# The first biases of a selective-attention kernel: two copies instead of one, a subtraction on GpSimd, and the first scores issued earlier

## The chip, the cores and the metric

The kernel runs on one core of one Trainium2 chip. The metric is the device time of one execution in microseconds (us). The core's engines are TensorE (PE in the profile; PEld is its weight load), VectorE (DVE), ScalarE (ACT), GpSimd (POOL) and SyncE (SP, which only issues DMAs here). Each works through its own instructions in program order, and they wait for each other by semaphores.

## What is computed

Two blocks follow each other. The first is causal attention with a learned decay: per batch and head the positive part of `s` is summed up along the sequence, and the difference of two sums is a bias on the score.

```python
B, H, S, D = 8, 8, 576, 64
scores = q @ k.transpose(0, 1, 3, 2) / np.sqrt(D)
cum = np.cumsum(np.maximum(s, 0.0), axis=-1)
bias = -(cum[:, :, :, None] - cum[:, :, None, :])
scores = np.where(causal, -1e9, scores + np.minimum(bias, 0.0))
attn = softmax(scores)
attn_out = attn @ v
```

The second block is a mixture of eight experts (512 to 1024 to 512, relu) on the 4608 tokens that the first yields; a gate decides per token whether it keeps the expert of the token before it.

## The kernel before

**Stages.** `attention` goes over 32 pairs of heads (8 batches with 4 pairs each), then `experts` goes over units of sorted tokens. The change lies in what `attention` does ahead of the loop and in the first turn of the loop.

**The bias.** Inside the softmax the part of the bias that depends on the query alone cancels, so the kernel adds only a term per key: `cum[key]` less the sum at a fixed middle column. There are two groups of queries (`GROUPS`: columns 0 to 320 and 320 to 576), each with a middle column of its own (`MIDS`), so that the exponents stay small. Lines 289 to 312 make all these terms once for all 64 heads: VectorE takes the positive part of `s` (L289), sums it up (L291), and subtracts the middle column for each group (`rel`, L299: 384 columns for the first group, 576 for the second). PE turns `rel` into columns of 128 keys (L302: three turnings for the first group, four for the second), and two small products (L307) put the last 64 keys, the tail, beside them. All of it goes into one PSUM tile `bps` (480 columns). One copy on VectorE (L310) brings it to `bias` in SBUF, and a memset (L312) masks half a block. ACT's exponentials (L339, L357) take columns of `bias` as their per-partition bias.

**PSUM.** The pool `ps_s` has three buffers of two banks (tag "s"). `bps` takes the first, and the scores of the units take them in turn. A buffer is taken again when what reads it is done.

**A pair.** `scores(n, u)` writes k q for one of three units (`UNITS`; each has 512 columns for each of two heads, L330). `weights` lets ACT take the exponentials of one piece of a unit into the SBUF tile `sc` (L339), and lets GpSimd zero what the causal mask hides (L345). `tail_scores` and `tail` (L351, L357) do the same for the last 64 keys; `seen_tail` (L361) masks them on VectorE. `gate_parts` (L370) and `beside_v` (L375, L376) put the gate's logits beside v. `rows` (L408 to L413) multiplies the weights of the pair before by v, and divides by the sum.

**Order.** The program's order is that of the Python code, written out by hand. Ahead of the loop it is: load pairs 0 to 2 (`load`, L255, issued on SP's queue, pair 0's k on ACT's), `spin(18)`, the bias, `tail_scores(0)`. `spin(n)` multiplies the identity by itself n times (L286) into a bank that nobody reads; each is two matmul records in the profile. In turn n of the loop: load pair n + 3, then for each unit its scores and its weights, then `rows(n - 1)` (in the first turn `spin(8)`), `tail_scores(n + 1)`, `gate_parts(n)`, `beside_v(n)`.

Of the kernel before, what the change touches and what calls it, by code (L numbers as in the profile page):

```python
# [10 lines left out]
F32 = mybir.dt.float32  # L11
I32 = mybir.dt.int32
Act = mybir.ActivationFunctionType
Alu = mybir.AluOpType
# [4 lines left out]
P = 128  # L19
B, H, S, DH = 8, 8, 576, 64  # L20
# [4 lines left out]
NPAIR = B * HP  # L25
NF = S // P
TS = NF * P
TL = S - TS
# [19 lines left out]
MASKED = -1e9  # L48
SUM_MIN, SUM_MAX = 1e-20, 1e20
GROUPS = ((0, 5 * TL), (5 * TL, S))  # L50
MIDS = (5 * TL // 2, 7 * TL)


UNITS = (
    ((0, 0, 0, 5 * TL), (3, 1, 3 * P, S)),
    ((0, 1, 5 * TL, S), (1, 1, 5 * TL, S)),
    ((2, 0, 2 * P, 5 * TL), (2, 1, 5 * TL, S), (1, 0, P, 5 * TL)),
)
# [9 lines left out]
def kernel(  # L68
# [33 lines left out]
    with ExitStack() as main:  # L102
# [51 lines left out]
        last = sort.group((6, 7), xs)  # L154

        attention(tc, q, kz, vz, vx, s, w_gate, w_local, ident, lg, recs, const, new_x, plan)
        tables = sort.tables()
        check = in_range(main.enter_context(tc.tile_pool(name="g_sb", bufs=1)), nc, recs, sort.total, sort.ones, out_of)
# [51 lines left out]
def attention(ctx, tc, q, kz, vz, vx, s, w_gate, w_local, ident, lg, recs, keep, new_x, plan):  # L210
# [14 lines left out]
    nc = tc.nc  # L225
    mm, tr = nc.tensor.matmul, nc.tensor.transpose
    scale = 1.0 / math.sqrt(DH)
    BH = B * H

    def pool(name, bufs, **kw):  # L230
        return ctx.enter_context(tc.tile_pool(name=name, bufs=bufs, **kw))
# [3 lines left out]
    once = pool("once", 1)  # L235
    ps_s = pool("ps_s", 3, space=PSUM)
# [3 lines left out]
    banks = [ps_o.tile([P, 512], F32, name=f"o{g}", tag=f"o{g}") for g in range(2)]  # L240
    COLUMNS = ((0, 3), (3, NB))
    TAIL = 2 * VW
# [3 lines left out]
    ins, raw, scs, xs = {}, {}, {}, {}  # L246

    def load(n, other=nc.sync):
        if n >= NPAIR:
            return  # L250
        b, hp = divmod(n, HP)
        ins[n] = [p_in.tile([P, S], F32, name="q"), *(p_in.tile([P, TS + 2 * TL], F32, name=x) for x in ("k", "vt")),
                  p_vx.tile([P, NB, VW], F32, name="v")]
        for t, x, eng in zip(ins[n], (q[b][:, hp], kz[n], vz[n], vx[n]), (nc.sync, other, nc.sync, nc.sync)):
            eng.dma_start(t, x)  # L255

    tmp = ctx.enter_context(ExitStack())
    t_in = tmp.enter_context(tc.tile_pool(name="t_in", bufs=1))
    s_sb = t_in.tile([BH, S], F32, name="s_sb")
# [3 lines left out]
    ones = t_in.tile([BH, S], F32, name="ones")  # L263
# [8 lines left out]
    for h in range(2):  # L272
        d = slice(h * DH, h * DH + DH)
# [5 lines left out]
    for h in range(2):  # L279
        d = slice(h * DH, h * DH + DH)  # L280
# [3 lines left out]
    def spin(n):  # L284
        for i in range(n):
            mm(banks[1][:, :P], lhsT=ident, rhs=ident, start=True, stop=True)  # L286

    spin(18)
    nc.vector.tensor_scalar_max(s_sb, s_sb, 0.0)  # L289
    cum = t_in.tile([BH, S], F32, name="cum")  # L290
    nc.vector.tensor_tensor_scan(cum, ones, s_sb, 0.0, op0=Alu.mult, op1=Alu.add)  # L291


    bps = ps_s.tile([P, 2, 512], F32, name="bps", tag="s")[:, 0]
    bias_of, at = {}, 0
    for g, (q0, q1) in enumerate(GROUPS):
        n = -(-q1 // P) * P if g == 0 else S
        rel = t_in.tile([BH, n], F32, name=f"rel{g}")
        nc.vector.tensor_scalar(rel, cum[:, :n], cum[:, MIDS[g] : MIDS[g] + 1], None, Alu.subtract)  # L299
        for c, a in enumerate(range(0, TS, P)):  # L300
            if a + P <= n:
                tr(bps[:, at : at + BH], rel[:, a : a + P], ident[:BH, :BH])  # L302
                bias_of[c, g] = at
                at += BH
    tail_bias = at
    for h in range(2):
        mm(bps[h * TL : h * TL + TL, at : at + NPAIR], lhsT=rel[:, TS:], rhs=ident[:BH, h:BH:2], start=True, stop=True)  # L307
    at += NPAIR
    bias = once.tile([P, at], F32, name="bias")
    nc.vector.tensor_copy(bias, bps[:, :at])  # L310
    at = bias_of[2, 0]
    nc.vector.memset(bias[TL:, at : at + BH], MASKED)  # L312
    tmp.close()
    p_sc = pool("p_sc", 2, reuse_waits="tile")

    def scores(n, u):

        qb, kb = ins[n][:2]
        ps = raw[u] = ps_s.tile([P, 2, 512], F32, name="ps", tag="s")
        scs[n, u] = p_sc.tile([P, 2, sum(z - a for _, _, a, z in UNITS[u])], F32, name=f"sc{u}")  # L320
        runs = []
        for c, g, a, z in UNITS[u]:
            if runs and runs[-1][0] == c and runs[-1][2] == a:
                runs[-1][2] = z
            else:
                runs.append([c, a, z, PIECE[c, g][1]])
        for c, a, z, at in runs:
            for h in range(2):
                d = slice(DH * h, DH * h + DH)
                mm(ps[:, h, at : at + z - a], lhsT=kb[d, c * P : c * P + P], rhs=qb[d, a:z],  # L330
                   start=True, stop=True)

    def weights(n, *pieces):

        for c, g in pieces:
            u, at, a, z = PIECE[c, g]
            for h in range(2):
                i = bias_of[c, g] + 2 * n + h
                nc.scalar.activation(scs[n, u][:, h, at : at + z - a], raw[u][:, h, at : at + z - a], Act.Exp,  # L339
                                     bias=bias[:, i : i + 1], scale=scale)  # L340
            if min(c * P + P, S) <= z and (c, g) in PIECE:
                at += c * P - a
                if at >= 0:
                    x = scs[n, u][:, :, at : at + P]
                    nc.gpsimd.affine_select(out=x, in_=x, compare_op=Alu.is_ge, fill=0.0, base=0,  # L345
                                            pattern=[[0, 2], [1, P]], channel_multiplier=-1)

    def tail_scores(n):
        for h in range(2):
            d = slice(DH * h, DH * h + DH)  # L350
            mm(banks[1][d, TAIL : TAIL + TL], lhsT=ins[n][1][:, TS:][:, d], rhs=ins[n][0][:, TS:], start=True, stop=True)  # L351

    def tail(n):

        sc = scs[n, "tail"] = p_sc.tile([P, TL], F32, name="tail")
        i = tail_bias + n
        nc.scalar.activation(sc, banks[1][:, TAIL : TAIL + TL], Act.Exp, bias=bias[:, i : i + 1], scale=scale)  # L357

    def seen_tail(n):
        x = scs[n, "tail"]  # L360
        nc.vector.scalar_tensor_tensor(x, x, 3e38, seen, Alu.min, Alu.mult)  # L361
# [3 lines left out]
    def gate_parts(n):  # L365

        m = P // 2
        for c in range(NB):
            for j in range(0, P, m):
                mm(gates[j : j + m, c], lhsT=ins[n][2][:, c * P + j : c * P + j + m], rhs=wz[:, n % HP],  # L370
                   start=True, stop=True)

    def beside_v(n):
        v = ins[n][3]
        nc.vector.tensor_copy(v[:, :, 1 : E + 2], gates[:, :, 0])  # L375
        nc.vector.tensor_copy(v[:, :, VW - E - 2 : VW - 1], gates[:, :, 1])  # L376
# [38 lines left out]
    def logits(b):  # L415
        x = xs.pop((b, "x"))
        for t0, t1, m in ((1, NB, P), (0, 1, TL)):
            part = x[:m, t0:t1, :XI].rearrange("p t (a w) -> p t a w", w=2 * HW)
            pair = keep.tile([P, NF, HP, E + 1], F32, name="pair")[:m, : t1 - t0]
            nc.vector.tensor_tensor(pair, part[:, :, :, : E + 1], part[:, :, :, 2 * HW - E - 1 :], op=Alu.add)  # L420
            nc.vector.tensor_reduce(lg[:m, b * NB + t0 : b * NB + t1, :], pair.rearrange("p t a e -> p t e a"),
                                    axis=AX, op=Alu.add)

    def bank(n):
        t = ps_s.tile([P, 2, 512], F32, name="bank", tag="s")
        return [t[:, i] for i in range(n)]

    tail_scores(0)
    for n in range(NPAIR + 1):
        load(n + 3)  # L430
        if n < NPAIR:
            for u, pieces in enumerate((((0, 0), (3, 1)), ((0, 1), (1, 1)), ((2, 0), (2, 1), (1, 0)))):
                scores(n, u)
                for piece in pieces:
                    weights(n, piece)
                    if piece == (0, 0):
                        tail(n)
                for f in plan.pop((n, 3 + u), ()):
                    f(bank)
            seen_tail(n)  # L440
        for f in plan.pop((n, 0), ()):
            f(bank)
        if n:
            rows(n - 1, 1)
            rows(n - 1, 0)
        else:
            spin(8)

        if n + 1 < NPAIR:
            tail_scores(n + 1)  # L450
        if n < NPAIR:
            gate_parts(n)
            beside_v(n)
        if n and n % HP == 0:
            logits(n // HP - 1)
        for half in (1, 2):
            for f in plan.pop((n, half), ()):
                f(bank)
# [899 lines left out]
```

## Time and profile before

| | us |
|---|---|
| median of 5 executions | 803.54 |
| lowest and highest of them | 801.27 and 804.6 |
| the profiled execution | 804.4 |
| its span, first to last instruction | 802.7 |
| PE busy | 784.6 |
| DVE busy | 338.7 |
| ACT busy | 237.0 |
| POOL busy | 175.1 |

How to read the lines: a group of instructions has its line in the source, its engine and operation, the tiles that it writes and reads (out<-in), shapes, count, busy time, the mean of one in ns, and the idle time of its engine just before, with what ended that. A timeline row has its start, its length, the same names, and in brackets the idle time before it. The chain of waits is the work that ended last, followed back from the end: each piece is what released the next one, or what stood before it on its engine. "issue" is time in which the profile shows nothing that was waited for.

### The profile page before, as it was taken

To read this page: it belongs to the slowest core of one execution; us is meant where nothing else is said; L and a number is where in the kernel's file an instruction comes from. 1 tells how busy PE (TensorE), PEld (TensorE's weight loads), DVE (VectorE), ACT (ScalarE), POOL (GpSimd) and SP (SyncE) were. 2 spreads that over 40 slices of the span, in tenths; PEclk is the share of its full clock that TensorE was granted. 3 is DMA by queue.
4 is the path that set the end of the run, shared out by engine and by line. 5 is a ranking of instruction groups with operands and counts; after the bars stand their busy time and mean duration, and the time that the engine had idled before them with its cause. 6 is when DMAs were issued, how large, how long until landed. Compare 5 with 4: busy or idle time off the path is not lost.

```text
span 802.7 us, 18230 instructions
## 1 busy us (share of the span) xinstructions
PE 784.6 (98%) x7078; PEld 562.5 (70%) x7078; DVE 338.7 (42%) x1228; ACT 237.0 (30%) x611; POOL 175.1 (22%) x329
## 2 busy tenths in 40 slices
PE   9999999999999989999999999999999999999996
PEld 8989888888788854863677537774477745676762
DVE  2233443444447658424372253622545225436000
ACT  5767766756654201111111111111111111111110
POOL 3423345454443141101110012101111011011001
PEclk9999999999999999999999999999999999999998
DMA  9486679887483389957999369993699946994001
GB/s 310 167 275 192 194 225 318 286 263 234 152 276 140 127 271 410 395 192 249 341 376 403 135 236 339 391 405 111 239 359 394 361 136 242 365 411 189 22 14 43
DMA packets 64146, 204.47 MB, mean 255 GB/s; under 512 B 8270, under 2 KB 8302, under 8 KB 64049
## 3 DMA queue, kind: packets, MB, share of 16 engines
q1 hardware_dynamic: 55008, 172.41, 60.6%
q0 software_dynamic: 8896, 30.47, 10.0%
q8 instruction: 58, 0.95, 0.5%
q10 hardware_dynamic: 144, 0.33, 0.2%
q14 instruction: 40, 0.32, 0.1%
HBM read 179.93 MB, written 23.76 MB: 254 GB/s over the span
## 4 chain that ended last, share of the span: by engine, by line
issue 57%; PE 29%; POOL 4%; DVE 4%; DMA 2%; POOLq 1%; another core or an unknown queue 1%; SPq 1%; ACT 0%; DVEq 0%
PE o L408 12%; PE ps L330 10%; POOL out_dram L1249 2%; PE o L370 2%; POOL xg L1184 2%; PE hp L1231 2%; DVE xT L1088 1%; DMA xg<-x_rows 1%; POOLq L1159 1%; SPq L808 1%; PE o L351 1%; DMA s_sb<-in_s_dram 1%; PE bank L947 1%; DVE x L413 0%
## 5 line engine op out<-in xcount | busy, mean ns | idle before, releaser
L1088 DVE STREAM_TRANSPOSE xT<-xg 32x128 f32<-32x128 f32 x576 | 174.2, 302 | 173.7 <-PE hp L1231 97.2
L1244 PE MATMUL yp<-w,hT 128*128 128x512 f32 (+1 forms) x528 | 218.0, 596 | 0.0
L1231 PE MATMUL hp<-xT,w 128*128 128x256 f32 (+1 forms) x1088 | 192.5, 337 | 3.3 <-issue 2.9
L1231 PEld LDWEIGHTS hp<-xT,w 128*128 128x128 f32 x1088 | 172.1, 191 | 27.5 <-issue 11.2
L339 ACT ACTIVATE sc<-ps,bias 128x256 f32<-128x256 f32 (+3 forms) x448 | 156.5, 482 | 62.7 <-PE ps L330 60.7
L1244 PEld LDWEIGHTS yp<-w,hT 128*128 128x128 f32 (+1 forms) x528 | 90.7, 181 | 115.7 <-issue 114.3
L1249 POOL DMA_INDIRECT out_dram<-y,at_gate x38 | 38.5, 1013 | 439.9 <-ACT y L1248 425.4
L408 PE MATMUL o<-v,sc 128*64 128x74 f32 x3072 | 118.8, 229 | 4.3 <-issue 3.8
L408 PEld LDWEIGHTS o<-v,sc 128*64 128x64 f32 x3072 | 111.2, 136 | 14.1 <-issue 10.6
L1235 ACT ACTIVATE hT<-hp 128x512 f32<-128x512 f32 x68 | 40.4, 597 | 195.7 <-PE hp L1231 183.3
L1248 ACT ACTIVATE y<-yp,at_gate 128x512 f32<-128x512 f32 x38 | 26.1, 687 | 240.8 <-PE yp L1244 234.6
L345 POOL TENSOR_SCALAR_AFFINE_SELECT sc<-sc 128x256 f32<-128x256 f32 x160 | 66.6, 420 | 132.1 <-ACT sc L339 69.4
L330 PE MATMUL ps<-q,k 64*128 64x320 f32 (+2 forms) x768 | 92.4, 386 | 0.2 <-issue 0.2
L330 PEld LDWEIGHTS ps<-q,k 64*128 64x128 f32 x768 | 69.6, 186 | 14.9 <-ACT r_v L957 0.6
L1244 PE MATMUL yp<-x,hT 128*128 128x512 f32 (+1 forms) x144 | 63.2, 594 | 0.0
L1222 DVE STREAM_TRANSPOSE hT<-x 32x256 f32<-32x256 f32 x64 | 27.9, 436 | 65.4 <-ACT x L1216 64.5
L410 DVE RECIPROCAL recs<-o 128x4 f32<-128x4 f32 x64 | 12.1, 189 | 93.6 <-PE o L408 78.7
L1231 PEld LDWEIGHTS hp<-xT,x 128*128 128x128 f32 x320 | 46.1, 191 | 5.8 <-issue 2.6
L1231 PE MATMUL hp<-xT,x 128*128 128x128 f32 (+1 forms) x320 | 50.1, 317 | 0.0
L1244 PEld LDWEIGHTS yp<-x,hT 128*128 128x128 f32 (+1 forms) x144 | 25.3, 178 | 26.2 <-issue 26.0
L1038 POOL DMA_INDIRECT x_rows<-x,r_slot_i x40 | 38.7, 968 | 9.3 <-issue 5.9
L413 DVE TENSOR_TENSOR x<-o,recs 128x292 f32<-128x292 f32 x64 | 34.5, 538 | 2.2
(163 smaller groups left out, 351.1 us busy)
## 6 DMA issues: line engine op xcount, KB each, us to landing
w<-in_w_dram SPq DMA_DIRECT2D x184, 512.0 KB
x<-in_w_dram SPq DMA_DIRECT2D x56, 512.0 KB
v<-in_vx_dram SPq DMA_DIRECT2D x32, 370.0 KB
vt<-in_vz_dram SPq DMA_DIRECT2D x32, 320.0 KB
k<-in_kz_dram SPq DMA_DIRECT2D x31, 320.0 KB
q<-in_q_dram SPq DMA_DIRECT2D x32, 288.0 KB
xg<-x_rows POOLq DMA_DIRECT2D x30, 293.0 KB
x_rows<-r_empty SPq DMA_DIRECT2D x6, 293.0 KB
```

The source lines that it names most:

```text
L330: mm(ps[:, h, at : at + z - a], lhsT=kb[d, c * P : c * P + P], rhs=qb[d, a:z], start=True, stop=True)
L339: nc.scalar.activation(scs[n, u][:, h, at : at + z - a], raw[u][:, h, at : at + z - a], Act.Exp, bias=bias[:, i : i + 1], scale=scale)
L345: nc.gpsimd.affine_select(out=x, in_=x, compare_op=Alu.is_ge, fill=0.0, base=0, pattern=[[0, 2], [1, P]], channel_multiplier=-1)
L408: mm(y, lhsT=w, rhs=x, start=start, stop=stop)
L413: nc.vector.tensor_tensor(x, y, rec.unsqueeze(3).to_broadcast([P, t1 - t0, 2, HW]), op=Alu.mult)
L1038: self.s.nc.gpsimd.indirect_dma_start(out=next(self.s.views)[:, :], out_offset=bass.IndirectOffsetOnAxis(ap=self.slot[:z, m : m + 1], axis=0),
L1088: self.nc.vector.transpose(self.xT[i][d : d + m, :, k * P + a * m : k * P + a * m + m], rows[a * m : a * m + m, :, X0 + d : X0 + d + m])
L1222: nc.vector.transpose(hT[i][d : d + m, :, a : a + m], x[a : a + m, :, d : d + m])
L1231: mm(y, lhsT=w[0][:, c, f : f + P], rhs=xT[i][:, c, :], start=(c == 0), stop=(c == DK - 1))
L1235: nc.scalar.activation(hT[i][:, g : g + per], ps, Act.Relu)
L1244: mm(ps[n * m : n * m + m, :], lhsT=hT[i][:, c, a : a + m], rhs=wn[:, c, :], start=(c == 0), stop=(c == FK - 1))
L1249: nc.gpsimd.indirect_dma_start(out=next(outs)[:, :], out_offset=bass.IndirectOffsetOnAxis(ap=at[i, k][:, 0:1], axis=0), in_=y[:, :], eleme ...
```

## The change

The change does five things.

1. The scores of the first pair's tail and of its first two units move in front of the turnings of the biases (PE's program order). The third unit's scores stay where they were.
2. `spin(18)` becomes `spin(11)`.
3. The second group's subtraction (64 partitions by 576 columns) goes from VectorE to GpSimd. Both subtractions get a second operation, a multiplication by 1.0.
4. The two groups are turned into the two banks of `bps`, and each bank is copied to `bias` by a copy of its own, 192 and 288 columns. The tail's terms are in the second one.
5. The tiles `sc` are taken from their pool in `weights`, in front of the first exponential of a unit, instead of in `scores`; the pool `p_sc` is still opened behind the biases.

```diff
-    spin(18)
-    nc.vector.tensor_scalar_max(s_sb, s_sb, 0.0)
-    cum = t_in.tile([BH, S], F32, name="cum")
-    nc.vector.tensor_tensor_scan(cum, ones, s_sb, 0.0, op0=Alu.mult, op1=Alu.add)
-    bps = ps_s.tile([P, 2, 512], F32, name="bps", tag="s")[:, 0]
-    bias_of, at = {}, 0
-    for g, (q0, q1) in enumerate(GROUPS):
...
-        nc.vector.tensor_scalar(rel, cum[:, :n], cum[:, MIDS[g] : MIDS[g] + 1], None, Alu.subtract)
...
-    bias = once.tile([P, at], F32, name="bias")
-    nc.vector.tensor_copy(bias, bps[:, :at])
...
     def scores(n, u):
...
-        scs[n, u] = p_sc.tile([P, 2, sum(z - a for _, _, a, z in UNITS[u])], F32, name=f"sc{u}")
...
+    spin(11)
+    nc.vector.tensor_scalar_max(s_sb, s_sb, 0.0)
+    cum = t_in.tile([BH, S], F32, name="cum")
+    nc.vector.tensor_tensor_scan(cum, ones, s_sb, 0.0, op0=Alu.mult, op1=Alu.add)
+    bps = ps_s.tile([P, 2, 512], F32, name="bps", tag="s")
+
+    tail_scores(0)
+    for u in range(2):
+        scores(0, u)
+
+    bias_of, width = {}, [0, 0]
+    for g, (q0, q1) in enumerate(GROUPS):
+        n = -(-q1 // P) * P if g == 0 else S
+        rel = t_in.tile([BH, n], F32, name=f"rel{g}")
+        (nc.gpsimd if g else nc.vector).tensor_scalar(rel, cum[:, :n], cum[:, MIDS[g] : MIDS[g] + 1], 1.0,
+                                                      Alu.subtract, Alu.mult)
+        for c, a in enumerate(range(0, TS, P)):
+            if a + P <= n:
+                tr(bps[:, g, width[g] : width[g] + BH], rel[:, a : a + P], ident[:BH, :BH])
+                bias_of[c, g] = width[0] * g + width[g]
+                width[g] += BH
+    tail_bias = sum(width)
+    for h in range(2):
+        mm(bps[h * TL : h * TL + TL, 1, width[1] : width[1] + NPAIR], lhsT=rel[:, TS:], rhs=ident[:BH, h:BH:2],
+           start=True, stop=True)
+    width[1] += NPAIR
+    bias = once.tile([P, sum(width)], F32, name="bias")
+    for g in range(2):
+        nc.vector.tensor_copy(bias[:, width[0] * g :][:, : width[g]], bps[:, g, : width[g]])
+    at = bias_of[2, 0]
+    nc.vector.memset(bias[TL:, at : at + BH], MASKED)
+    tmp.close()
+    p_sc = pool("p_sc", 2, reuse_waits="tile")
+
     def weights(n, *pieces):
         for c, g in pieces:
             u, at, a, z = PIECE[c, g]
+            if (n, u) not in scs:
+                scs[n, u] = p_sc.tile([P, 2, sum(z - a for _, _, a, z in UNITS[u])], F32, name=f"sc{u}")
...
-    tail_scores(0)
     for n in range(NPAIR + 1):
...
-                scores(n, u)
+                if n or u == 2:
+                    scores(n, u)
```

More of the change, by code (lines that the diff above doesn't have):

```diff
@@ L286, in spin @@
             mm(banks[1][:, :P], lhsT=ident, rhs=ident, start=True, stop=True)
-    spin(18)
-    nc.vector.tensor_scalar_max(s_sb, s_sb, 0.0)
-    cum = t_in.tile([BH, S], F32, name="cum")
-    nc.vector.tensor_tensor_scan(cum, ones, s_sb, 0.0, op0=Alu.mult, op1=Alu.add)
-    bps = ps_s.tile([P, 2, 512], F32, name="bps", tag="s")[:, 0]
-    bias_of, at = {}, 0
-    for g, (q0, q1) in enumerate(GROUPS):
[L297 to L308, printed above, removed]
-    bias = once.tile([P, at], F32, name="bias")
[L310 to L314, printed above, removed]
     def scores(n, u):
@@ L331, in scores, with tail_scores @@
                    start=True, stop=True)
+    def tail_scores(n):
+        for h in range(2):
+            d = slice(DH * h, DH * h + DH)
+            mm(banks[1][d, TAIL : TAIL + TL], lhsT=ins[n][1][:, TS:][:, d], rhs=ins[n][0][:, TS:], start=True, stop=True)
+    spin(11)
[18 more added lines that the diff above has]
+    tail_bias = sum(width)
+    for h in range(2):
+        mm(bps[h * TL : h * TL + TL, 1, width[1] : width[1] + NPAIR], lhsT=rel[:, TS:], rhs=ident[:BH, h:BH:2],
[8 more added lines that the diff above has]
+    p_sc = pool("p_sc", 2, reuse_waits="tile")
     def weights(n, *pieces):
@@ L346, in weights @@
                                             pattern=[[0, 2], [1, P]], channel_multiplier=-1)
[L348 to L351, printed above, removed]
     def tail(n):
```

## The prediction

> **What bounds the kernel now.** I read the page first, then the chain of waits over the first 30 us, then the timeline of that stretch. The page says which engine's time is the kernel's time:
>
> ```profile
> PE 784.6 (98%) x7078; PEld 562.5 (70%) x7078; DVE 338.7 (42%) x1228; ACT 237.0 (30%) x611; POOL 175.1 (22%) x329
> ```
>
> TensorE is busy for 784.6 of 802.7 us. The list of PE's waits holds nothing of this size but the start (1.6 us) and some called "issue" (7.5 us together), so what PE stops doing at the start, or waits for there, moves all that follows. The chain of waits in the first pair (start us, duration us, what):
>
> ```profile
> 5.80 0.46 DVE s_sb L289
> 6.28 1.36 DVE cum L291
> 7.67 0.42 DVE rel L299
> 8.14 0.40 PE bps L302 x3
> 8.57 0.46 PE bps L302 x4
> 9.02 0.23 PE bps L307 x4
> 9.26 0.27 PE o L351 x4
> 9.53 2.79 PE ps L330 x24
> 12.32 1.98 PE o L286 x16
> ```
>
> The reader is to see that nothing of q and k (L351, L330) runs on PE until the biases are turned: PE spins, waits for rel, turns, and only then scores. The first pair's scores end at 12.32 us; this is the mark that I compare.
>
> ```profile
> 1.55 6.41 PE L286 MATMUL o<-ident 128*128 128x128 f32 x36 [1.55 <-POOL ident masks.py:199]
> ...
> 7.67 0.84 DVE L299 TENSOR_SCALAR rel<-cum 64x384 f32<-64x384 f32 x2
> ...
> 8.14 0.89 PE L302 MATMUL bps<-ident,rel 64*128 64x64 f32 x7 [0.17 <-DVE rel L299]
> ...
> 9.31 0.66 DVE L310 COPY bias<-bps 128x480 f32<-128x480 f32 x1 [0.80 <-PE bps L307]
> ...
> 10.69 0.95 ACT L339 ACTIVATE sc<-ps,bias 128x320 f32<-128x320 f32 x2 [7.81 <-PE ps L330]
> ```
>
> Each line of spin is two matmul records. PE waits 0.17 us for the first rel, and the first exponential (ACT, 10.69) waits for PE, 0.7 us after the biases lie in SBUF.
>
> **The change, part by part.**
>
> *Seven spins less.* The timeline of 0 to 6.1 us alone reads
>
> ```profile
> 1.55 4.74 PE L286 MATMUL o<-ident 128*128 128x128 f32 x21 [1.55 <-POOL ident masks.py:199]
> ```
>
> so 21 of the 36 records end at 6.29 and the other 15 need 7.96 - 6.29 = 1.67 us, 0.11 each. The 14 that go are of these: 14 x 0.111 = 1.56 us. The 22 left end at 6.40.
>
> *Scores in front of the turnings.* They now need q and k of pair 0. The SP queue's waits show landings in their order: pair 2's q (issued 5.79) went out on the landing of s, pair 2's k (issued 6.21) on the next one in line, which I take for pair 0's q: landed at 6.2, k earlier. That is an inference from the order, with only 0.2 us to spare; I count no wait. The tail's scores take 0.27 (L351): 6.67. Each of the three units has 512 columns for each of two heads, so a third of L330's 2.79 us, 0.93: two units end at 8.53. By then the first rel (done at 7.67 + 0.41 = 8.08) waits for PE, and the old wait of 0.17 is gone. Three turnings, pipelined behind the scores, some 0.25: 8.78.
>
> *The second subtraction on GpSimd.* It starts at 7.70, when cum is there; POOL has stood idle since 5.38 and is next wanted by the first pair's masks, which wait for ACT. No row shows a POOL subtraction of 576 columns. The nearest rows (line, shape, count, busy, mean ns):
>
> ```profile
> L345 POOL TENSOR_SCALAR_AFFINE_SELECT sc<-sc 128x256 f32<-128x256 f32 x160 | 66.6, 420 | 132.1 <-ACT sc L339 69.4 <-issue 52.1 <-PE ps L330 7.7
> ...
> L791 POOL MEMSET r_empty<- 128x586 f32 x1 | 0.6, 586 | 0.0
> ...
> L777 POOL TENSOR_SCALAR r_low<-r_lane 128x8 f32<-128x8 f32 x1 | 0.2, 195 | 0.1
> ```
>
> The select of 256 columns takes 0.42 and that of 64 columns (L281) 0.23, 0.97 ns a column: 0.73 for 576. The memset of 586 takes 0.59 and reads nothing. I take 0.70, bounds 0.59 and 1.46 (twice the select's). It runs beside VectorE's own subtraction (0.41), and there the trace has a warning. A select that started at 89.51, beside a VectorE scan with two inputs, took 0.83 us instead of 0.41 (min, median and max of the selects stand in the second line), so it ended 0.39 us after the scan:
>
> ```profile
> 88.60 1.35 DVE L961 TENSOR_TENSOR_SCAN r_v<-r_u,r_v 2x576 f32<-2x576 f32 x1 [0.21 <-ACT r_v L957]
> ```
> ```profile
> L345 POOL TENSOR_SCALAR_AFFINE_SELECT sc<-sc x160: 399/408/830, 11.8 to 253.1; 128x256 f32<-128x256 f32 x160
> ```
>
> So I let POOL's 0.70 begin when VectorE's 0.41 ends: rel for group 2 at 8.08 + 0.70 = 8.78, and PE's turnings of it at 8.83 (0.05 is what PE needed after rel before). Unblocked and at 0.59 it is there at 8.29 and PE never waits.
>
> The Trainium skill, "SBUF — State Buffer", section "Who interferes with whom", speaks against this part of the change: GpSimd and VectorE share a port pair, a float32 tensor_scalar can run in a mode that takes both ports, and the second to issue is blocked for the whole of the first. The two rel rows fit such a mode (411 and 505 ns, 0.49 ns a column, against 1.05 for the copy out of PSUM); no run here shows the pair of instructions side by side. By the rule the sum is the 1.2 us below, without it 1.5.
>
> *Turning and copying apart.* Before, turnings of group 2 plus the tail's biases took 8.57 to 9.26, 0.69: now 8.83 to 9.52. The copies: 480 columns took 0.658, 45 columns (L375) 0.206, 1.04 ns a column, so 0.36 for the first 192 columns and 0.46 for the other 288. The first copy lies beside PE's work (8.83 to 9.19). The second runs 9.57 to 10.03. **This one is on the path**: there are three score buffers, bps holds one, units 0 and 1 the others, so unit 2's scores must wait for the second copy. Before, the same buffer was free at 9.97 and wanted at 12.32 - 0.93 = 11.39, and the copy was hidden. Now PE stands from 9.52 to 10.08, a new hole of 0.56 us. Queued behind it on PE: unit 2, the eight spins, pair 1's tail scores. Unit 2 then ends at 10.08 + 0.93 + 0.1 (filling an idle PE) = 11.11.
>
> **Sum**: 12.32 - 11.11 = 1.2 us earlier (1.56 + 0.17 + about 0.1 gained, 0.56 + 0.1 lost). With the low bound for POOL, PE turns through to 9.26, copy to 9.77, unit 2 ends at 10.85: 1.5. With the high bound, rel at 9.54, unit 2 at 11.9: 0.4.
>
> *ACT.* Its first exponential can start at 9.2 instead of 10.69; a pair takes it 10.69 to 15.69, 5.0 us. Pair 1's unit 2 needs the buffer that ACT empties last, at 16.97 (third third of L330's 15.11 to 17.90), so 15.77 after the shift; ACT is done at 14.3. If the first exponential waits for the second copy and the memset behind it (0.11), it starts at 10.2 and ends at 15.2: still covered. The moved p_sc buffers are asked for by the same engine in the same order; I cost that at nothing, covered by the same 0.5 us.
>
> *After the first pair* all hangs on PE: SP's queue waits for PE (108 us for score and gate matmuls, 208 for yp), and by the same order of SP's issues the inputs of pair 1 land by 12.7, the k among them by 10.9; q and k are wanted at 13.0 (L351 at 14.23, less 1.2), v long after. No DMA is moved. So the shift should reach the end whole: the profiled execution, 804.4 us about a span of 802.7, becomes 803.2; the median of the five runs shown, 803.54, lies 0.86 below it, and becomes **802.3**.
>
> **Rivals.**
> 1. *The landing of q takes the place of the turnings.* Against: the order of landings. For: only 0.2 us to spare, where there were 3. Each 0.1 us later costs 0.1; a landing at 7.0 leaves 0.6 of the gain: 803.0.
> 2. *Split copy does nothing for ACT* (the first exponential waits for the whole bias tile): the change then doesn't do what it says, but ACT is covered, so 802.3 still.
> 3. *The shift recuts a stall further on.* The windows (us, then busy PE, PEld, DVE, ACT, POOL, then granted clock):
>
> ```profile
> 251.79:255.21 3.42, 2.76 (x86) 2.69 (x83) 2.61 (x10) 1.22 (x4) 1.04 (x4) 1.00 0.16 16
> ...
> 289.35:292.76 3.41, 0.73 (x3) 0.69 (x4) 0.66 (x4) 0.32 (x1) 0.55 (x1) 1.00 0.76 276
> 292.76:296.17 3.41, 3.41 (x6) 1.38 (x5) 2.96 (x20) 1.25 (x3) 0.00 (x0) 0.50 0.58 106
> ```
>
> PE stood for 2.7 of 3.41 us, and the next 3.41 us ran at half clock: 1.7 us lost. The hole of 0.66 in the first line cost no clock, so mine of 0.56 won't. If the stall at 289 falls otherwise, 1.7 comes on top: 803.54 - 2.9 = 800.6. "TensorE: Matmul & The Clock Gate", Part 1, says that the gate looks at free-running windows of 3413 ns; by it a shift of 1.2 us can split that stall over two windows, and an unlucky one can lose as much.
> 4. *Slower: the hole at unit 2.* POOL's subtraction feeds the second copy, and PE waits for that. At 1.9 us for it the gain is gone; at 3.5 us the hole is 3.4 us, unit 2 ends at 13.9, 1.6 late, and half a clock for 3.41 us costs 1.7 more: 806.8. For it: no POOL row of this kind and size. Against: 3.5 us is nearly five times what the select's slope gives.
>
> **How the numbers follow.** Forecast (gain 0.4 to 1.5) 0.62; rival 1 0.07; rival 2 0.10 (same time); rival 3 0.15; rival 4 0.06. The measurement can tell about 0.3%, 2.4 us. Only rival 3 is faster by more (0.15), only rival 4 slower by more (0.06), the rest, 0.79, is within. Range: from 800.3 (gain 1.5 and 1.7 at the stall) to 804.0 (the forecast, and 1.7 lost there); rival 4 is left out.
>
> **What would show it.** Right: 22 spin records; L351 near 6.3 with no wait; L302 without a wait for the first group; a PE gap of about half a microsecond before the third unit, ended by DVE's second copy; POOL's subtraction near 1.1 us long, blocked included; the first exponential near 9.2; pair 1's scores about 1.2 us earlier than 15.04, and the same lead at 250 us and at the end. Wrong: a wait for q or k before L351; a hole over 1 us; a lead that shrinks between the first and the fourth pair; or a stall near 288 us of other length.

## The result, and the profile after

The changed kernel takes 806.42 us (median of 51 executions, 802.48 to 813.4), the kernel before 804.02 us on the same chips (93 executions, 801.1 to 810.19). The ratio is 1.0035, with a 95% interval of 1.0026 to 1.0045: slower by 2.1 to 3.6 us. The forecast was 1.2 us faster.

The profiled execution of the changed kernel took 808.56 us, span 807.0, at a mean granted clock of 0.989 (before: 804.4, 802.7 and 0.995). The page's first line:

```profile
PE 786.8 (97%) x7064; PEld 562.8 (70%) x7064; DVE 338.1 (42%) x1228; ACT 237.0 (29%) x611; POOL 177.7 (22%) x330
```

PE executes 14 matmuls less and is busy 2.2 us longer: some of its work ran slower. The timeline of the start, in order of time (start us, length us, what, idle time before it and what ended that):

```profile
1.55 4.10 PE L286 MATMUL o<-ident 128*128 128x128 f32 x22 [1.55 <-POOL ident masks.py:199]
...
6.75 0.34 PE L307 MATMUL o<-q,k 128*64 128x64 f32 x4 [1.09 <-DMA q<-in_q_dram]
...
7.01 2.00 PE L301 MATMUL ps<-q,k 64*128 64x320 f32 x16
...
7.49 0.41 DVE L324 TENSOR_SCALAR rel<-cum 64x384 f32<-64x384 f32 x1
7.56 2.44 POOL L324 TENSOR_SCALAR rel<-cum 64x576 f32<-64x576 f32 x1 [2.20 <-DVE cum L312]
...
8.85 0.34 PE L328 MATMUL bps<-ident,rel 64*128 64x64 f32 x3
...
10.05 0.46 PE L328 MATMUL bps<-ident,rel 64*128 64x64 f32 x4 [0.86 <-POOL rel L324]
...
10.44 0.30 PE L333 MATMUL bps<-ident,rel 64*64 64x32 f32 x4
...
10.79 0.72 DVE L338 COPY bias<-bps 128x192 f32<-128x192 f32 x2 [2.88 <-PE bps L333]
...
11.25 0.95 ACT L352 ACTIVATE sc<-ps,bias 128x320 f32<-128x320 f32 x2 [8.38 <-DVE bias L338]
...
11.66 2.08 PE L301 MATMUL ps<-q,k 64*128 64x320 f32 x8 [0.92 <-DVE bias L338]
...
13.66 3.78 PE L286 MATMUL o<-ident 128*128 128x128 f32 x16
...
17.37 0.48 PE L307 MATMUL o<-q,k 128*64 128x64 f32 x4
```

Four things are to be seen. POOL's subtraction takes 2.44 us where 0.70 was counted. PE stands three times: 1.09 us for the landing of q, 0.86 for POOL, 0.92 for VectorE's copies; before, it stood 0.17 us in all. The first copy, of 192 columns that PE had turned by 9.19, starts at 10.79, when the second group and the tail are turned too (L333 done at 10.74). And the eight spins (16 matmuls) take 3.78 us, where this view has 2.05 before (1.98 in the chain of waits). The windows of PE say why (stretch, length, busy PE, granted clock, DMA share, GB/s):

```profile
4.48:7.89 3.41, 2.32 (x23) 1.00 0.94 264
7.89:11.30 3.41, 1.99 (x23) 1.00 1.06 331
11.30:14.72 3.42, 3.06 (x13) 0.50 1.04 392
14.72:18.13 3.41, 3.41 (x27) 0.50 1.04 401
```

The stretches are laid along the edges at which the clock changed. At 4.48 the matmuls of the spins, 0.21 us apart until then, came to lie 0.11 us apart; below, this is called the rise of the clock. It is read from this spacing: the granted clock of the profile says 1.00 on both sides of it. At 11.30 the granted clock fell. In the stretch before that PE was idle for 3.41 - 1.99 = 1.42 us, and the next two ran at half clock.

The mark of the prediction, the end of unit 2, is 11.66 + 2.08 = 13.74 instead of 12.32; pair 1's tail scores start at 17.37 instead of 14.23, 3.14 us late. The lag reaches the end, but it is not one constant shift: pair 1's first scores are 3.47 us late (18.51 for 15.04), those near 60 us only 2.18 (60.10 for 57.92; before, PE stood for 0.58 us just ahead of them, and after the change it doesn't), and at the last pair of the attention it is 3.3 again (257.63 for 254.31 where PE comes back from 0.66 us of idle time), as at the stall near 292 us (296.23 for 292.90). Stalls on the way move it by about 1 us either way. There this execution lost 1 us more: the half clock that follows the stall lasted for two stretches (294.61 to 301.44) where before it lasted for one. The last matmul ends 4.3 us late.

### The profile page after: what moved, and what is told of

It reads as the page before. It is cut to its first block, busy times and chain, and to the rows that moved or that the text cites. A ratio compares the mean times of both kernels' runs of the same rounds, so it can differ in the third digit from the quotient of the medians.

```text
span 807.0 us, 18206 instructions
## 1 busy us (share of the span) xinstructions
PE 786.8 (97%) x7064; PEld 562.8 (70%) x7064; DVE 338.1 (42%) x1228; ACT 237.0 (29%) x611; POOL 177.7 (22%) x330
## 4 chain that ended last, share of the span: by engine, by line
issue 57%; POOL 4%; POOLq 1%; DMA 0%; SPq 0%
POOL out_dram L1257 2%; POOL xg L1192 2%; POOLq L1167 1%; DMA x_rows<-r_empty 0%; POOLq L1192 0%; POOLq L1257 0%; POOL xg L1188 0%; SPq L812 0%; POOLq L1188 0%; POOLq L166 0%; SPq L816 0%
```

## The experiments

Three questions are asked. Why does the subtraction cost 2.44 us: is that its own price, or is it blocked by VectorE beside it, or a first call? Where is the loss made: in the path through POOL and the copies, in the scores in front of the turnings (q's landing), or in the clock? And is the rest of the change worth anything without POOL? Each run is set against the kernel before on the same chip; that takes 789 us on two of the chips used here and 801 to 804 on the third, so times are compared on one chip only. The start of the trace scatters too: pair 1's tail scores begin at 14.23 in the trace of the kernel before, and at 13.80 and 14.50 in e4_price and e11_price2, which leave its first pair as it is.

**e1_dve: the change with VectorE's subtraction.**

```diff
-        (nc.gpsimd if g else nc.vector).tensor_scalar(rel, cum[:, :n], cum[:, MIDS[g] : MIDS[g] + 1], 1.0,
+        nc.vector.tensor_scalar(rel, cum[:, :n], cum[:, MIDS[g] : MIDS[g] + 1], 1.0,
```

> The changed kernel with the second group's subtraction back on VectorE, nothing else. Theory P (GpSimd's subtraction, 2.44 us in the changed kernel where I had put 0.70, opens the hole in the turnings): the second rel is there at about 8.4 us, the wait of 0.86 before the second turnings is gone, the third unit's scores end about 11.2 us, and the time is 0.8 to 1.2 us below the kernel before (ratio 0.9985 to 0.999). Rival Q (the wait for pair 0's q, 1.09 us, and the wait for the second copy, 0.92, are enough to lose the gain and the clock): the time stays within 0.8 us of the changed kernel, 2 us or more above the kernel before (ratio 1.002 or more).

Measured: 788.1 against 789.11 us, ratio 0.9994 (0.9974 to 1.0014). Timeline of its start:

```profile
7.40 0.84 DVE L324 TENSOR_SCALAR rel<-cum 64x384 f32<-64x384 f32 x2
...
8.80 0.59 PE L328 MATMUL bps<-ident,rel 64*128 64x64 f32 x7
...
9.67 0.72 DVE L338 COPY bias<-bps 128x192 f32<-128x192 f32 x2 [1.43 <-PE bps L333]
...
10.54 1.13 PE L301 MATMUL ps<-q,k 64*128 64x320 f32 x8 [0.92 <-DVE bias L338]
```

All seven turnings run through, unit 2 starts 1.1 us earlier than with POOL, the clock stays full, and pair 1's tail scores start at 13.58: 0.65 us ahead of the trace of the kernel before, but only 0.22 ahead of the same start on this chip (13.80 in e4_price). Unit 2 ends at 11.67, not at the 11.2 that was expected. The hole of 0.92 in front of unit 2 is there without POOL too: both copies still stand in it. So the change without GpSimd shows no loss here, and gains no more than can be measured.

**e3_pool: the kernel before, with only the second subtraction on GpSimd.**

```diff
-        nc.vector.tensor_scalar(rel, cum[:, :n], cum[:, MIDS[g] : MIDS[g] + 1], None, Alu.subtract)
+        (nc.gpsimd if g else nc.vector).tensor_scalar(rel, cum[:, :n], cum[:, MIDS[g] : MIDS[g] + 1], 1.0,
+                                                      Alu.subtract, Alu.mult)
```

> The kernel before with one part of the change alone: the second group's subtraction on GpSimd (both subtractions with the second operation). Theory P: GpSimd takes about 2.4 us again, the second turnings start near 10.1 instead of 8.57, the third unit ends 1.6 us later, and PE stands for 1.6 us in one piece: ratio 1.0015 to 1.002 if the clock holds, up to 1.004 where it falls. Rival (GpSimd was slow in the changed kernel only because of what ran beside it there): about 0.7 to 1.1 us for the subtraction and a ratio within 1.0005.

Measured: 791.49 against 789.11 us, ratio 1.0033 (1.002 to 1.0047). POOL's subtraction takes 2.44 us again, and PE waits 1.59 us for it:

```profile
7.48 2.44 POOL L299 TENSOR_SCALAR rel<-cum 64x576 f32<-64x576 f32 x1 [2.12 <-DVE cum L291]
...
7.99 0.40 PE L303 MATMUL bps<-ident,rel 64*128 64x64 f32 x3
...
9.97 0.46 PE L303 MATMUL bps<-ident,rel 64*128 64x64 f32 x4 [1.59 <-POOL rel L299]
```

Pair 1's tail scores start at 15.63, against 13.80 in e4_price, whose first pair is that of the kernel before: 1.8 us. The mean granted clock was 0.997 or more in all five executions, as in nearly all of the kernel before on that chip. This one part, alone, makes the kernel slower by as much as the whole change does (1.6 to 3.7 us here), with no help of the clock.

**e4_price: the price of the subtraction by itself.** The kernel before, with seven more GpSimd subtractions on a small tile, away from the first pair.

```diff
+        def probe(z, m, ptr):
+            def go(bank):
+                nc.gpsimd.tensor_scalar(flat[:z, :m], flat[:z, :m], flat[:z, :1] if ptr else 0.0, 1.0, Alu.subtract, Alu.mult)
+            return go
```

> The kernel before with seven subtractions of this kind more on GpSimd, spread over pairs 1 to 3, on a tile of zeros that they leave as it is: 64 partitions by 360 columns twice, by 180 and by 72 with the scalar read per partition from SBUF, 128 by 360 the same, and 64 by 360 and by 180 with the scalar as a constant. Theory P1 (GpSimd's price per column): about 3.5 ns a column, 1.3 us for 360, whichever scalar, 0.7 for 180. Theory P2 (the scalar from SBUF is what costs): 1.3 us with it, 0.5 with a constant. Theory P3 (VectorE's own subtraction beside it blocked it, or the first call was slow): 0.5 us for 360 columns, or only the first of the two equal ones long. The time itself says nothing, since the added work delays the masks behind it.

Measured (the groups of POOL by line, shapes kept apart: busy us, mean ns of one, idle time before):

```profile
L138 POOL TENSOR_SCALAR lg<-lg 64x360 f32<-64x360 f32 x3 | 4.4, 1466 | 0.1
L138 POOL TENSOR_SCALAR lg<-lg 64x180 f32<-64x180 f32 x2 | 1.7, 846 | 0.2
L138 POOL TENSOR_SCALAR lg<-lg 128x360 f32<-128x360 f32 x1 | 1.5, 1501 | 0.1
...
L138 POOL TENSOR_SCALAR lg<-lg 64x72 f32<-64x72 f32 x1 | 0.5, 525 | 0.0
```

The two of 64x360 that subtract a column took 1.49 and 1.50, the one that subtracts a constant 1.41. From 72 to 360 columns it is (1.494 - 0.525) / 288 = 3.4 ns a column, the same for 64 and 128 partitions, and the second call is as long as the first. Worked out for 576 columns: 0.525 + 504 x 3.36 ns = 2.22 us. So nearly all of the price is the operation's own, and not a block or a first call; if the slope holds up to 576 columns, what VectorE's 0.41 beside it can have added is 2.44 - 2.22 = 0.2 us. The Trainium skill, "GPSIMD Engine Reference", section 4.1, has one-input elementwise work on GpSimd at roughly line rate, and its section 3.1 has 1.03 cycles an element for up to two operations; at the 1.2 GHz of that section this would be an estimated 0.86 ns a column. The select of this kernel (0.97 ns a column) is near that, the subtraction is four times as dear, and the measurement decides.

**e11_price2: which part of it is dear.** As e4_price, with three other operations on the same tile:

```diff
+            nc.gpsimd.tensor_scalar(again, again, flat[:64, :1], None, Alu.subtract)
...
+            nc.gpsimd.tensor_copy(flat[:64, :180], flat[:64, 180:])
...
+            nc.gpsimd.tensor_tensor(flat[:64, :180], flat[:64, :180], flat[:64, 180:], op=Alu.add)
```

> The kernel before with three GpSimd operations more, on a tile of zeros that they leave as it is: a subtraction of 64 by 360 with a scalar per partition and no second operation, a copy of 64 by 180, and a sum of two tiles of 64 by 180. If the second operation (times 1.0) is what makes the subtraction slow: 0.5 to 0.8 us for the first. If it is GpSimd's tensor-with-scalar arithmetic as such: 1.5 us, as with the second operation. For the copy I expect 0.35 us (the casts' 0.75 to 0.84 ns a column); for the sum no row bears on it, 0.4 to 0.9 us.

Measured, in the same view:

```profile
L138 POOL TENSOR_SCALAR lg<-lg 64x360 f32<-64x360 f32 x1 | 1.2, 1191 | 0.0
...
L144 POOL TENSOR_TENSOR lg<-lg 64x180 f32<-64x180 f32 x1 | 0.6, 557 | 0.1
...
L141 POOL COPY lg<-lg 64x180 f32<-64x180 f32 x1 | 0.3, 328 | 0.0
```

Without the multiplication by 1.0 a subtraction of 360 columns takes 1.19 instead of 1.49 us: the second operation is a fifth of the price, and the result lies between the two that were expected. A copy of 180 columns takes 0.33, a sum of two tiles 0.56, the subtraction with two operations 0.88 (in e4_price, with a column as its scalar). So neither the select nor a memset could have stood for it.

**e6_inloop: does the first copy wait because of where it stands?** Both subtractions on VectorE, and each copy in the loop, behind its own group's turnings:

```diff
+    bias = once.tile([P, 3 * BH + 4 * BH + NPAIR], F32, name="bias")
...
+        if g:
+            tail_bias = sum(width)
...
-    for g in range(2):
```

> The changed kernel with the second subtraction on VectorE and each group's copy issued right behind its turnings, in front of the next group's. Theory S (the first copy waited because it stands behind the second group's turnings in the program, and waits for the last write to the tile): the first copy starts about 0.1 us after the third turning, the hole in front of the third unit falls from 0.92 to 0.5 to 0.6 us, and the first exponential starts before the second copy ends. Rival (the tile is tracked as a whole): the second group's turnings now wait for the first copy, 0.4 us, and the hole moves instead of shrinking.

One execution: 792.7 us against a median of 789.12. The timeline:

```profile
9.09 0.36 DVE L338 COPY bias<-bps 128x192 f32<-128x192 f32 x1 [0.74 <-PE bps L329]
...
9.36 0.50 DVE L325 TENSOR_SCALAR rel<-cum 64x576 f32<-64x576 f32 x1
...
9.54 0.95 ACT L352 ACTIVATE sc<-ps,bias 128x320 f32<-128x320 f32 x2 [6.67 <-DVE bias L338]
...
9.92 0.46 PE L329 MATMUL bps<-ident,rel 64*128 64x64 f32 x4 [0.87 <-DVE rel L325]
...
11.17 1.28 PE L301 MATMUL ps<-q,k 64*128 64x320 f32 x8 [0.56 <-DVE bias L338]
```

The first copy now starts 0.04 us behind its third turning, the first exponential begins in front of the second copy, and the hole in front of unit 2 falls from 0.92 to 0.56 us. So it is the place in the program that held the copy back in the change: there both copies stand behind all the turnings, and the first one waits for L333. Here the copy stood in VectorE's queue in front of the second subtraction and delayed that; PE waited 0.87 us for it, and the clock fell from 12.03 to 15.45.

**e2_fill, e7_fill2: PE kept busy.** The change with more spins ahead and some between the two groups' turnings; e2_fill has four more ahead of unit 2.

```diff
-    spin(11)
+    spin(16)
...
+        if g:
+            spin(4)
...
+                if n == 0 and u == 2:
+                    spin(4)
```

> The changed kernel with 13 more spins, which lie in the three places where PE waited: 16 instead of 11 at the start (up to the landing of q), 4 between the two groups' turnings, 4 in front of the third unit's scores. They add 2.8 us of PE work and take no wait away. Theory C (most of the loss is the clock, which falls to half for 6.83 us because PE stood still for 1.4 of the 3.41 us before it): the clock stays full at the start, and the time falls to within 0.8 us of the kernel before (ratio 0.999 to 1.001), although there is more work. Rival H (the holes themselves are the loss, and the clock would have fallen anyway): the time stays where the changed kernel is or above it (ratio 1.0025 or more).

> The changed kernel with spins only where PE waited for q (16 instead of 11) and for GpSimd's subtraction (4 between the two groups' turnings); none in front of the third unit, where the spins of an earlier run had to wait for ACT's reading of the same bank. GpSimd's 2.44 us stay. Theory C (the clock is most of the loss): the clock stays full for the first 20 us and the time is at most 0.1% above the kernel before (0.9995 to 1.001), 2 us below the unchanged variant in the same job. Rival H (the late second turnings and what hangs on them are the loss): the same ratio as the unchanged variant, 1.0025 to 1.0045.

Measured: e2_fill 793.2 against 789.11, ratio 1.0061 (1.004 to 1.0081); e7_fill2, without the last two lines, 791.12 against 789.12, 1.0024 (1.0012 to 1.0035). In e2_fill the spins ahead of unit 2 had a wait of their own, since they write the bank in which ACT was still reading the tail's scores:

```profile
12.69 1.16 PE L286 MATMUL o<-ident 128*128 128x128 f32 x8 [1.70 <-ACT tail L367]
```

So e2_fill tells nothing of the clock. e7_fill2 had a mean granted clock of 0.997 or more in all 11 executions and was slower all the same, by 0.9 to 2.8 us: in its trace the clock rose late, at 7.71 us, the 32 matmuls of its 16 spins lasted until 8.31, and unit 2 began at 13.31. Theory C, which expected at most 0.1% above the kernel before, missed here.

**e5_same, e13_same: the changed kernel again, beside others.**

> The changed kernel as it is, beside its own variants on one chip. Both theories: ratio 1.0025 to 1.0045, as measured. Theory C (clock): where the granted clock of the profile falls to half in the first 20 us, pair 1's tail scores come near 17.4 us; where it stays full they come near 14, as on the chip of the first trace the time lost before the clock fell was only 0.3 us.

> The changed kernel once more, beside the two variants that take one loss each away, all on one chip. Ratio 1.0025 to 1.0045. Theory C: its executions fall in two groups by granted clock, those at 0.997 or more within 1 us of the kernel before, the others 3 us or more above it. Theory P alone: one group, all about 2.5 us above.

Measured: e5_same 791.5 against 789.12, ratio 1.0032 (1.0016 to 1.0049); e13_same 806.23 against 803.71, 1.0027 (1.0004 to 1.0051). The eleven executions of e5_same fall into two groups. Five with a mean granted clock of 0.998 or more took 789.14 to 790.81 us (median 789.37, 0.3 above the kernel before); six at 0.995 or less took 791.5 to 794.83 (median 793.75, 4.6 above it). Of the 29 executions of the kernel before, 28 were at 0.997 or more. In the profiled execution of e5_same q had landed in time, and PE's windows are

```profile
9.37:12.78 3.41, 1.81 (x17) 1.00 1.04 377
12.78:16.19 3.41, 3.41 (x17) 0.50 1.04 400
16.19:19.60 3.41, 3.41 (x48) 1.00 1.04 395
```

1.60 us idle in one stretch, half a clock in the next. But the start isn't all that this execution (793.42 us) loses: its pair 1 begins the tail scores at 16.34, e7_fill2's (791.9 us, same chip, no half clock at the start) at 16.35, and yet its last matmul ends 1.7 us later, at 784.99 for 783.25. So the 4.6 us of those six can't all be put down to the clock of the start. On the chip of e13_same the clock of the whole execution doesn't sort the executions, because there the kernel before loses clock near 290 us too.

**e9_gap, e14_gap: the change with PE busy only while it waits for POOL.**

```diff
+        if g:
+            spin(4)
```

> The changed kernel with 4 spins between the two groups' turnings and nothing else; they fit in the time in which PE waits for GpSimd's subtraction there (0.86 to 1.33 us), so the order of arrival behind them is the same. Theory C (idle time of about 1.4 us or more within one 3.41 us stretch halves the clock for the next): at most 1.1 us is left idle in one stretch, the clock falls in few executions (granted clock 0.997 or more in at least 9 of 11), and the time is 0 to 1 us above the kernel before (ratio 1.000 to 1.0012). Rival H (the late arrival of the second turnings is the loss): ratio 1.0025 to 1.0045 as in the unchanged kernel.

> The changed kernel with 4 spins in the time in which PE waits for GpSimd's subtraction. Theory C: few executions in the group of low clock, median 1 us or more below the unchanged kernel on this chip, 0.3 to 1 us above the kernel before. Theory P alone: as the unchanged kernel, within 0.6 us.

Measured: e9_gap 803.17 against 801.47, ratio 1.0022 (1.0002 to 1.0041); e14_gap 804.96 against 803.71, 1.002 (1.0001 to 1.0039). The start keeps its clock: at most 0.94 and 1.09 us idle in a stretch; pair 1's tail scores at 14.81 and 14.65 instead of 17.37 and (e13_same) 17.58. By times e13_same is 1.3 us above e14_gap, on one chip, with intervals that overlap. Theory C's expectation for e9_gap was missed: 7 of 12 executions had a granted clock of 0.997 or more, not 9 of 11, and the ratio is above its 1.0012.

**e10_spin18: the change with the old number of spins.**

```diff
-    spin(11)
+    spin(18)
```

> The changed kernel with 18 spins at the start again, as before the change. PE then comes to the second turnings at 10 to 10.9 us, about when GpSimd has done, and only the wait for the copies (0.92 us) is left. Theory C: the seven spins that were cut gained nothing, since GpSimd's 2.44 us set the time behind them, but they kept the clock: granted clock 0.997 or more in at least 9 of 11 executions, ratio 1.0004 to 1.0015, less than the unchanged kernel's 1.003. Rival H (the path alone): each spin is 0.11 us of PE work, so the time rises above the unchanged kernel, ratio 1.0035 or more.

Measured: 802.69 against 801.47, ratio 1.0016 (1.0002 to 1.0031). Spins and scores now fill PE until the subtraction is done, so that neither q nor POOL is waited for; unit 2 starts at 11.38, 0.28 earlier than with 11 spins, as much as the subtraction began earlier here (7.28 for 7.56), and pair 1's tail scores start at 14.43:

```profile
11.38 1.13 PE L301 MATMUL ps<-q,k 64*128 64x320 f32 x8 [0.92 <-DVE bias L338]
```

The seven spins taken out bought nothing, since the path runs through POOL. A stretch near 290 us of this run was some 1.5 us idle, and the next one was at full clock: idle time of a stretch alone is not the whole rule.

**e15_dve: e1_dve again, beside e13_same and e14_gap.**

> The changed kernel with the second subtraction on VectorE. Theory P: 2.5 us or more below the unchanged kernel on this chip and 0 to 1.2 us below the kernel before (ratio 0.9985 to 1.0), with hardly an execution of low clock. Rival Q (the wait for q and for the copies is enough): within 1 us of the unchanged kernel.

Measured: 804.74 against 803.71, ratio 1.0013 (1.0 to 1.0027). It is 1.5 us below e13_same, less than expected, and not below the kernel before: its clock rose only at 7.72 us, and pair 1's tail scores start at 14.01, 0.5 ahead of the start of the kernel before on this chip where its clock rose as late (14.50 in e11_price2).

**e8_order, e12_order12: another order.** VectorE's subtractions, the turnings between unit 0 and unit 1, and fewer spins:

```diff
-    spin(11)
+    spin(16)
...
-    for u in range(2):
-        scores(0, u)
+    scores(0, 0)
...
+    scores(0, 1)
...
-            spin(8)
+            spin(4)
```

e12_order12 differs from e8_order by `spin(12)`.

> A version built from what the runs show: both subtractions on VectorE, 16 spins at the start, the turnings between the first and the second unit's scores, so that the second unit covers both copies, and 4 instead of 8 spins behind the first pair's scores, since ACT starts earlier. Theory P and S: no wait in front of the third unit, its scores end near 10.9 to 11.1 us, pair 1's tail scores start 1.5 to 2 us ahead of the kernel before; ratio 0.9970 to 0.9985. Rival (something behind the first pair takes the lead back: ACT's 5.0 us for a pair, or the landing of pair 1's k near 11): pair 1's third unit waits for ACT, and the ratio is 0.999 or more.

> The version with both subtractions on VectorE, the turnings between the first and the second unit, and 4 spins behind the first pair, now with 12 instead of 16 spins at the start, because 16 outlast the landing of q wherever the clock rises late. Pair 1's tail scores start 1.5 to 2 us ahead of the kernel before, no hole above 1.1 us in one stretch of 3.41 us: ratio 0.9975 to 0.9990. Rival (the lead of the first pair is lost to stalls that fall otherwise in every execution further on, or the clock falls at the start for want of spins): 0.9995 or more.

Measured: e8_order 788.57 against 789.12, ratio 0.9999 (0.9985 to 1.0012), pair 1's tail scores at 12.46. e12_order12: **799.62 against 801.47, ratio 0.9977 (0.9961 to 0.9993)**, faster than the kernel before, and so than the changed one, which lost in all three of its comparisons. Its timeline:

```profile
6.42 1.14 PE L301 MATMUL ps<-q,k 64*128 64x320 f32 x8
7.13 0.84 DVE L323 TENSOR_SCALAR rel<-cum 64x384 f32<-64x384 f32 x2
...
7.60 0.89 PE L327 MATMUL bps<-ident,rel 64*128 64x64 f32 x7
...
8.65 2.12 PE L301 MATMUL ps<-q,k 64*128 64x256 f32 x16
8.77 0.72 DVE L337 COPY bias<-bps 128x192 f32<-128x192 f32 x2 [0.80 <-PE bps L332]
...
11.79 0.34 PE L307 MATMUL o<-q,k 128*64 128x64 f32 x4
```

Unit 0 covers the subtractions, unit 1 covers the copies (8.77 to 9.49, while PE is at units 1 and 2 from 8.65 to 10.77), and PE waits for neither. Pair 1's tail scores come 2.4 us ahead of the trace of the kernel before (2.7 ahead of e11_price2, on the same chip, whose clock rose late); the median is 1.9 us lower. Of the 2.4, 0.9 are the four spins fewer behind the first pair (1.16 us for 2.05), so the order and the shorter start have 1.5. That e8_order, 1.8 us ahead of that trace (none of the kernel before was taken on its chip), isn't faster by its times is not explained.

## Why the prediction was wrong, point by point

**The step that failed** is the price of the second subtraction: "I take 0.70, bounds 0.59 and 1.46 (twice the select's)". It measured 2.44 us in the change (2.43 to 2.44 in every run that has it), and 2.22 follows from its own slope. The select and the memset share POOL with it and nothing else; a bound of twice the select's was no bound. Put into the prediction's own working from the measured start of 7.56, 2.44 gives rel at 10.00, turned by 10.74, copied by 11.25, and unit 2 done at 12.33: just the 12.32 of before. So this size alone takes the whole gain, as rival 4's "At 1.9 us for it the gain is gone" has it (1.9 counted from 8.08 is 9.98). Of the block that the prediction allowed for (POOL begins when VectorE ends) little can have been there: POOL's row starts at 7.56, beside VectorE's 7.49 to 7.90; a full block would take 0.34 us of it, and 0.2 is all that the slope leaves.

**The first copy beside PE's work** failed too: "The first copy lies beside PE's work (8.83 to 9.19)". It stood behind L333 instead and added itself to the hole: 0.92 for 0.56, so 0.36 us. e6_inloop shows that the place in the program did it. 1.22 us (rel at 10.00 for 8.78) and 0.36 make unit 2 start at 11.66 for 10.08.

**The clock.** "The hole of 0.66 in the first line cost no clock, so mine of 0.56 won't" judged one hole. Here three waits came together to 2.9 us, 1.42 of idle time fell into one stretch of 3.41 us, and the clock fell behind it. With half a clock unit 2 took 2.08 for the 1.03 counted, and the spins 3.78 for 2.05. At full clock the 3.05 us that e10_spin18 has from unit 2's start to pair 1's tail scores would put those at 11.66 + 3.05 = 14.71: so of the 3.14 us of lag in the trace 0.5 is the path, and 2.7 is the clock. The two groups of e5_same point the same way (0.3 and 4.6 us, part of it lost later), e9_gap and e14_gap, whose traces keep the clock at the start and which still lose 1.2 to 1.7 us in the median, less so. What share of the loss in the median is the clock's is not settled, and it isn't lost in every execution.

**The landing of q**: "I count no wait" missed 1.09 us here. PE went on with q at 6.75, not 6.2; and the spins ended at 5.65, not 6.40, because the clock rose at 4.48 instead of 6.04. The first group's turnings came at 8.85 for 8.53. That moved nothing by itself, as PE stood for POOL afterwards until 10.05, but the idle time was there for the clock. In e5_same there was no such wait.

**What held**: the first group's turnings without a wait; the hole in front of unit 2, ended by VectorE's copy, as the new limit; ACT off the path although its first exponential came at 11.25 instead of 9.2; a shift at the start that reaches the end, though moved by the stalls between; and rival 4, which named the place, the break-even and the half clock, and was given 0.06 on the ground that 3.5 us were far from the select's slope.

## What to carry to other kernels

Don't price an operation that the trace lacks by another kind of operation on the same engine: a probe of two sizes costs one run, and without one the chance of the dear end has to be large. When one long wait is split into several short ones, add up their idle time within a stretch of the clock, not each for itself. A copy that is to overlap with later work on the same tile has to stand in front of that work in the program; and before moving work to another engine, try an order in which the work that is there covers it, as in e12_order12.

## What the runs showed of the hardware

- GpSimd's float32 subtraction with a multiplication takes 3.4 ns a column, for 64 and for 128 partitions, with a column or a constant as its scalar; its select takes 0.97, and VectorE's subtraction 0.49.
- The clock at the start halved after stretches of 3.41 us with 1.42, 1.43, 1.60 and 1.70 us idle (the change, e6_inloop, e5_same, e13_same), and stayed full where no stretch had more than 0.91 to 1.26 us (e1_dve, e2_fill, e3_pool, e7_fill2, e9_gap, e10_spin18, e14_gap, e15_dve). Further on idle time doesn't sort the stretches: 1.41 us in e14_gap (291.38 to 294.79) and some 1.5 in e10_spin18 and e12_order12 halved nothing, while in e14_gap the clock fell at 192.39 after a stretch with 0.43 us idle. What else decides is open. The Trainium skill, "TensorE: Matmul & The Clock Gate", Part 1, has the half rate come after an idle window of some 3.4 us; here a partly idle one was enough.
- The half clock lasted for a second stretch where the first of them had 0.36 or 0.61 us idle (the change, e13_same), and for one only where it had none (e5_same, e6_inloop). That isn't a rule either: near 298 us of e13_same the first had 0.72 idle, and there was no second.
- The stretches lie on a grid: in the kernel before, the fall at 292.76 comes 84 stretches of 3.413 us after the rise at 6.04.
- The first rise of the clock, read from the spacing of the matmuls, came anywhere from 4.43 to 7.72 us between runs of nearly the same start. A spin's matmul takes 0.21 us before it and 0.11 after, so a fixed number of spins ends at a time that is not fixed.
